# The descriptor space of GpSimd's transfers, 4096 bytes a partition, in a convolution and mixture-of-experts kernel

## The chip, the cores and the metric

The kernel runs on one core of one Trainium2 chip. The metric is the device time of one execution in microseconds (us). Before the change it is 1196.7 us, the median of 3 runs (1196.11 to 1197.26).

## What is computed

The reference chains two parts. The first is a dynamic convolution over 8 sequences of 3584 tokens with 192 values each: every token has 8 heads with 7 weights each, the weights go through a softmax, and each head of 24 values becomes the weighted sum of the token's own values and those of the 6 tokens before it. The second is a mixture of experts with one expert for each token, cut here to what matters:

```
logits = normalized(x) @ normalized(expert_emb).T / tau      # 28672 tokens, 8 experts
expert_idx = argmax(logits); gate_w = its softmax value
for e in range(8):
    h = maximum(x[expert_idx == e] @ w1[e], 0)                # 192 -> 1024
    out[expert_idx == e] = gate_w * (h @ w2[e])               # 1024 -> 192
```

Inputs and output are float32: 8 matrices w1 of 192 x 1024, 8 matrices w2 of 1024 x 192, and an output of 28672 rows of 192 values (768 bytes).

## The kernel before

The tokens are taken in 32 units of 896 (128 partitions by 7). For each unit VectorE forms the convolution's products and sums, ScalarE scales and splits the result into two float16 parts, and SP turns it by a DMA transpose, so that PE can form the logits. VectorE then chooses an expert for each token and counts places, and GpSimd scatters the rows to `lst`, a list in DRAM that has a region for each expert (`scatter`, line 629): one indirect DMA for each of a unit's 7 columns, 128 rows of 776 bytes, 224 such transfers in all.

The experts' layers run over tiles of 256 or 128 rows of one expert. SP fetches a tile's rows from `lst` by a DMA transpose, PE multiplies them with w1 into `h_ps`, ScalarE and VectorE make two float16 parts of the result (`hi`, `lo`), PE multiplies these with w2 into `acc`, and ScalarE scales the sum with the gate into `o`. GpSimd then stores 128 rows of 768 bytes to the output by an indirect DMA (`store`, line 804), 228 transfers in all.

GpSimd also loads the experts' weights at the start (`load`, line 269): four transfers for each expert, of which the fourth, w2, lands as 8 pieces of 768 bytes in each of 128 partitions. With 8 experts these are 32 transfers. The program lets 8 transfers of GpSimd stand open at a time: each one waits on the semaphore of the one 8 before it, unless something else has already waited for that.

```
G_.dma_start(out=self.wa, in_=w1[e, 0:P, :]),
G_.dma_start(out=self.wb[0:D2, :], in_=w1[e, P:D, :]),
G_.dma_start(out=self.wb[D2 : 2 * D2, :], in_=w1[e, P:D, :]),
G_.dma_start(out=self.wc, in_=w2[e].rearrange("(c p) d -> p c d", p=P)),
```

The order of all this on each engine is set before the program is built, by a planner with a cost for each step (`run_steps`). The last 28 tiles take what is left of each expert's rows. Behind them the program computes how many rows are still left and branches (line 1622: `with tc.If(some > 0)`); in this data none are left, and the loops inside are skipped. At the end of that branch the semaphores are set back, GpSimd's own transfers among them (INC_SWDGE_SEM), and at the end of the program (line 1668, `with _tile.TileContext(nc)`) each engine runs a DRAIN and a barrier. Line 1655 makes the program's object; what stands there in the trace is the program's opening, with the same two kinds of instruction.

A transfer that GpSimd issues is written by GpSimd itself, as descriptors, into a space in SBUF that the program sets aside; SP's transfers don't use it. The size of the space is an argument of the program's object; where nothing is given, the library takes 16384 bytes in each partition.

## Time and profile before

| | before |
|---|---|
| median of 3 runs | 1196.7 us (1196.11 to 1197.26) |
| profiled execution | 1197.47 us |
| its span, first to last instruction | 1195.4 us |
| PE (matmul) busy | 1112.6 us, 93% |
| VectorE busy | 1034.4 us, 87% |
| ScalarE busy | 811.0 us, 68% |
| GpSimd busy | 623.7 us, 52% |
| mean granted TensorE clock | 0.976 of full speed |

The page counts what an engine does with data as busy. Register, branch, semaphore and drain instructions are not in these numbers, nor in the list of the costliest groups; they show up where a line's instructions are listed one kind at a time, with a q behind the engine's name (POOLq is GpSimd's, SPq is SP's queue). POOL is GpSimd, DVE is VectorE, ACT is ScalarE. A matmul's line is L66 throughout, that of a helper which records all operations, so groups are told apart by their tiles' names.

### The profile page before, as it was taken

What the parts mean: (1) busy time and instruction counts of PE and PEld (TensorE: products, weight loads), DVE (VectorE), ACT (ScalarE), POOL (GpSimd) and SP (SyncE); (2) the same over time, 40 slices, a digit from 0 to 9 for tenths busy, and PEclk for the clock granted to TensorE, in tenths of its full rate; (3) what the DMA queues carried; (4) which work ended last, traced back from release to release, by engine and by line L of the source; (5) the groups of instructions that cost most, each with busy time, mean ns of one, the idle gap of its engine ahead of it and who ended that gap; (6) DMA issues with size and microseconds to landing.
All of it is one profiled execution on the core that took longest, in us unless ns stands there. A gap on an engine that the chain in (4) does not pass through costs nothing.

```text
span 1195.4 us, 34677 instructions
## 1 busy us (share of the span) xinstructions
PE 1112.6 (93%) x13318; PEld 982.1 (82%) x13318; DVE 1034.4 (87%) x1561; ACT 811.0 (68%) x2076; POOL 623.7 (52%) x566
## 2 busy tenths in 40 slices
PE   4888698679999999999999999999999999999994
PEld 2444487568898899889988989989999988999994
DVE  8999999999999999999999999999984362358882
ACT  1678687669898987988888676776665444444442
POOL 4136262827566685856668675738564632223231
PEclk9988899979999999999999999999999999999998
DMA  9989364566676567755766564744444412211110
GB/s 237 284 172 215 105 158 107 155 139 151 161 164 164 137 162 156 183 153 130 162 158 157 139 159 119 157 116 135 97 97 114 131 49 50 48 43 47 46 45 23
DMA packets 254495, 156.15 MB, mean 131 GB/s; under 512 B 225005, under 2 KB 238565, under 8 KB 251248
## 3 DMA queue, kind: packets, MB, share of 16 engines
q1 hardware_dynamic: 228656, 94.86, 36.9%
q0 software_dynamic: 25664, 58.98, 16.7%
q8 instruction: 106, 1.74, 0.6%
q14 instruction: 69, 0.57, 0.2%
HBM read 62.20 MB, written 46.45 MB: 91 GB/s over the span
## 4 chain that ended last, share of the span: by engine, by line
PE 78%; DVE 12%; issue 3%; DMA 2%; ACT 2%; POOL 1%; DVEq 0%; POOLq 0%; SPq 0%; ACTq 0%
PE h_ps L66 40%; PE acc L66 35%; DVE acc_0x L66 3%; DVE prod_1x L66 2%; DVE prod_0x L66 2%; DVE acc_1x L66 2%; DMA w_t<-in_weight_gen_dram 2%; PE g_ps L66 1%; PE sums_a L66 1%; DMA wlast<-in_moe_w_dram 1%; DVE sums L66 1%; POOL lst L66 1%; ACT hi L66 1%; DVE w_t L66 0%; DVE wall L66 0%
## 5 line engine op out<-in xcount | busy, mean ns | idle before, releaser
L66 POOL DMA_INDIRECT out_dram<-o,meta x228 | 298.3, 1308 | 335.6 <-ACT o L66 192.3
L66 PE MATMUL h_ps<-xt,wall 128*128 128x128 f16 (+2 forms) x5120 | 461.2, 251 | 7.8 <-DVE sums L66 3.4
L66 PEld LDWEIGHTS <-wall 128*128 128x128 f16 (+2 forms) x5316 | 386.0, 98 | 85.7 <-issue 38.0
L66 PE MATMUL acc<-wall,hi 128*128 128x192 f16 x3200 | 411.2, 247 | 0.0
L66 PE MATMUL acc<-wall,lo 128*128 128x192 f16 x1600 | 395.1, 247 | 2.0 <-ACT lo L66 1.9
L66 PEld LDWEIGHTS <-hi 128*128 128x128 f16 x3648 | 328.8, 98 | 11.0 <-issue 3.2
L66 ACT ACTIVATE hi<-h_ps 128x512 f16<-128x512 f32 x456 | 259.3, 598 | 106.3 <-PE h_ps L66 101.1
L66 DVE SCALAR_TENSOR_TENSOR lo<-h_ps,hi 128x512 f16<-128x512 f32 x236 | 154.6, 685 | 109.1 <-ACT hi L66 107.6
L66 ACT ACTIVATE o<-acc,meta 128x192 f32<-128x192 f32 x228 | 88.0, 418 | 166.7 <-issue 148.1
L66 PEld LDWEIGHTS <-lo 128*128 128x128 f16 x1824 | 178.5, 98 | 3.1 <-ACT lo L66 3.1
L66 DVE TENSOR_TENSOR prod_1x<-x_t,w_t 128x1344 f32<-128x1344 f32 x93 | 144.0, 1548 | 0.0
L66 DVE TENSOR_TENSOR prod_0x<-x_t,w_t 128x1344 f32<-128x1344 f32 x93 | 143.9, 1547 | 0.0
L66 ACT ACTIVATE lo<-h_ps 128x512 f16<-128x512 f32 x220 | 127.4, 600 | 10.6 <-PE h_ps L66 8.8
L66 POOL DMA_INDIRECT lst<-row_0x,pos x77 | 102.0, 1324 | 58.0 <-issue 27.8
L66 POOL DMA_INDIRECT lst<-row_1x,pos x77 | 104.9, 1362 | 35.2 <-issue 29.4
L66 POOL DMA_INDIRECT lst<-row_2x,pos x70 | 88.5, 1264 | 48.5 <-issue 47.4
L66 PE MATMUL h_ps<-hi,minus 128*128 128x512 f16 x220 | 72.9, 379 | 7.5 <-ACT hi L66 7.3
L66 DVE TENSOR_TENSOR acc_0x<-acc_0x,prod_1x 128x1344 f32<-128x1344 f32 x45 | 69.8, 1550 | 0.5
L66 DVE TENSOR_TENSOR acc_1x<-acc_1x,prod_1x 128x1344 f32<-128x1344 f32 x45 | 69.6, 1548 | 0.5
L66 DVE TENSOR_TENSOR acc_0x<-acc_0x,prod_0x 128x1344 f32<-128x1344 f32 x45 | 69.8, 1550 | 0.0
L66 DVE TENSOR_TENSOR acc_1x<-acc_1x,prod_0x 128x1344 f32<-128x1344 f32 x45 | 69.6, 1548 | 0.0
L66 PEld LDWEIGHTS <-xT 128*128 128x128 f16 (+1 forms) x918 | 27.8, 97 | 26.4 <-DMA xT<-row_1x 11.8
(217 smaller groups left out, 1365.5 us busy)
## 6 DMA issues: line engine op xcount, KB each, us to landing
x_t<-in_x_dram SPq DMA_DIRECT2D x24, 1248.0 KB
w_t<-in_weight_gen_dram SPq DMA_DIRECT2D x16, 392.0 KB
x_t<-in_x_dram SPq DMA_DIRECT2D x8, 672.0 KB
wall<-in_moe_w_dram POOLq DMA_DIRECT2D x7, 768.0 KB
x_t<-in_x_dram SPq DMA_DIRECT2D x8, 504.0 KB
out_dram<-o,meta POOLq DMA_INDIRECT x228
wall<-in_moe_w_dram POOLq DMA_DIRECT2D x7, 512.0 KB
wall<-in_moe_w_dram POOLq DMA_DIRECT2D x14, 256.0 KB
```

Source lines behind the costliest of these rows:

```text
L66: self.last = self.tc.keep_in_program_order(op(*args, **kwargs))
```

## The change

One argument is given where the program's object is made. All instructions stay as they are, in the same order on each engine; every tile in SBUF starts 12288 bytes lower, since the space lies ahead of the tiles (the first tile's address goes from 16384 to 4096).

```
-    nc = _bacc.Bacc("TRN2", target_bir_lowering=False, num_devices=1)
+    nc = _bacc.Bacc("TRN2", target_bir_lowering=False, num_devices=1, dynamic_dma_scratch_size=4096)
```

## Rows read from the trace of the kernel before

**Rows 1.** The page: span, and busy time of each engine (share of the span)

```profile
span 1195.4 us, 34677 instructions
...
PE 1112.6 (93%) x13318; PEld 982.1 (82%) x13318; DVE 1034.4 (87%) x1561; ACT 811.0 (68%) x2076; POOL 623.7 (52%) x566
```

**Rows 2.** Timeline at the end: start us, us, engine line op out<-in [idle before]

```profile
1179.34 0.42 ACT L66 ACTIVATE o<-acc,meta 128x192 f32<-128x192 f32 x1 [1.38 <-issue]
1180.04 0.97 POOL L66 DMA_INDIRECT out_dram<-o,meta  x1 [1.01 <-ACT o L66]
```

**Rows 3.** Windows of the tail: length, busy us by engine, PEclk, DMA share, GB/s

```profile
1181.10:1183.90 2.80, 0.00 (x0) 0.00 (x0) 0.00 (x0) 0.00 (x0) 0.00 (x0) 0.92 0.14 39
1183.90:1186.10 2.20, 0.00 (x0) 0.00 (x0) 0.00 (x0) 0.00 (x0) 0.00 (x0) 0.50 0.01 4
1186.10:1194.60 8.50, 0.00 (x0) 0.00 (x0) 0.00 (x0) 0.00 (x0) 0.00 (x0) 0.50 0.00 0
```

**Rows 4.** Line 1622: ns min/median/max, first and last start us

```profile
L1622 POOLq INC_SWDGE_SEM  x1: 2240/2240/2240, 1183.9 to 1183.9; - x1
```

**Rows 5.** Line 1668, the program's end

```profile
L1668 SPq EVENT_SEMAPHORE  x14: 17/28/28, 1186.0 to 1195.3; - x14
L1668 POOLq EVENT_SEMAPHORE  x4: 17/17/17, 1194.6 to 1195.3; - x4
L1668 POOLq DRAIN  x3: 46/103/8402, 1186.1 to 1195.1; - x3
L1668 SPq DRAIN  x3: 7/7/13, 1186.8 to 1194.8; - x3
...
L1668 PEldq DRAIN  x2: 8/8/8, 1183.1 to 1194.9; - x2
```

**Rows 6.** Waits of SP's queue from 1170 us on: us, times, longest

```profile
SPq L1668 <- PEq L1668: 8.4, 2, 7.9
```

**Rows 7.** Line 1655, the program's opening

```profile
L1655 POOLq INC_SWDGE_SEM  x1: 27/27/27, 0.1 to 0.1; - x1
...
L1655 POOLq DRAIN  x1: 183/183/183, 0.3 to 0.3; - x1
```

**Rows 8.** Groups of GpSimd: xcount, busy us, mean ns, idle before

```profile
L66 POOL DMA_INDIRECT out_dram<-o,meta x228 | 298.3, 1308 | 335.6 <-ACT o L66 192.3 <-ACT meta L66 72.6 <-issue 15.4
L66 POOL DMA_INDIRECT lst<-row_1x,pos x77 | 104.9, 1362 | 35.2 <-issue 29.4 <-ACT row_2x L66 4.4 <-DVE lo L66 1.1
L66 POOL DMA_INDIRECT lst<-row_0x,pos x77 | 102.0, 1324 | 58.0 <-issue 27.8 <-DVE row_0x L66 17.4 <-ACT wall L66 12.7
L66 POOL DMA_INDIRECT lst<-row_2x,pos x70 | 88.5, 1264 | 48.5 <-issue 47.4 <-DMA lst<-row_1x,pos 0.3 <-ACT sq L66 0.3
L66 POOL DMA_DIRECT2D wall<-in_moe_w_dram x28 | 18.1, 651 | 45.9 <-DMA wall<-in_moe_w_dram 24.6 <-DMA xT<-row_0x 21.3
L66 POOL DMA_DIRECT2D wlast<-in_moe_w_dram x4 | 2.5, 663 | 0.0
```

**Rows 9.** Timeline of GpSimd, an early stretch and a late one

```profile
153.15 1.28 POOL L66 DMA_INDIRECT out_dram<-o,meta  x1 [0.30 <-issue]
155.25 0.97 POOL L66 DMA_INDIRECT out_dram<-o,meta  x1 [0.82 <-ACT o L66]
...
902.29 0.97 POOL L66 DMA_INDIRECT out_dram<-o,meta  x1 [0.30 <-ACT hi L66]
903.56 0.97 POOL L66 DMA_INDIRECT lst<-row_2x,pos  x1 [0.30 <-issue]
```

**Rows 10.** The output's stores: ns min/median/max, first and last start us

```profile
L66 POOL DMA_INDIRECT out_dram<-o,meta x228: 967/1163/2378, 153.2 to 1180.0; - x114
```

**Rows 11.** Waits of GpSimd: us in total, times, longest

```profile
POOL wall L66 <- DMA wall<-in_moe_w_dram: 24.6, 12, 6.3
```

**Rows 12.** Timeline of GpSimd, the first weight loads

```profile
7.43 5.36 POOL L66 DMA_DIRECT2D wall<-in_moe_w_dram  x8
19.06 0.55 POOL L66 DMA_DIRECT2D wall<-in_moe_w_dram  x1 [6.26 <-DMA wall<-in_moe_w_dram]
```

## The prediction

> **What bounds the kernel now.** I read four views, in this order. First the span and the page's busy times. They give a span of 1195.4 us and a PE that is busy for 93% of it [rows 1]; from here to the last stores the kernel is a PE kernel, and GpSimd, the only engine whose transfers the change touches, is busy 52% of the time. A change to GpSimd's transfers therefore gains nothing in the middle, unless it changes what PE waits for. Second, the timeline of the last microseconds: the last store to the output, a GpSimd transfer, starts at 1180.04 and takes 0.97 us [rows 2]. The span ends 14.4 us after that. Third, the windows of this tail: from 1181.1 on no engine is busy, and after 1186.1 the DMA engines move nothing either [rows 3]. The reader is to see that this is no wait for data. Fourth, the queue instructions of the two lines that stand there. On line 1622 GpSimd runs one INC_SWDGE_SEM of 2240 ns from 1183.9 [rows 4]. On line 1668 it runs three DRAINs of 46, 103 and 8402 ns, the first from 1186.1 [rows 5]; a DRAIN of 8.4 us that started later than that would end after the span, so the long one is the first, from 1186.1 to 1194.5. GpSimd's own barrier semaphores start at 1194.6 [rows 5], and SP, whose own DRAIN started at 1186.8, sits there for 7.9 us [rows 5, 6]; the view of waits puts that down to PE, whose DRAIN had begun at 1183.1 [rows 5], so it must be GpSimd. So 2.24 + 8.40 = 10.6 us of the 14.4 us tail are two GpSimd instructions of bookkeeping, with everything else waiting.
>
> The same two instructions stand at the start of the program, before the first transfer. There INC_SWDGE_SEM takes 27 ns and GpSimd's DRAIN 183 ns [rows 7]. Between the two places lie 228 + 77 + 77 + 70 + 28 + 4 = 484 transfers of GpSimd [rows 8]. What these have left behind is 8402 - 183 = 8219 ns of DRAIN and 2240 - 27 = 2213 ns of INC_SWDGE_SEM. It is not data under way: nothing moves in that window [rows 3].
>
> **The change part by part.** No instruction is added, removed or moved; on every engine the two programs have the same instructions in the same order. Two things differ: the space that GpSimd keeps its transfers' descriptors in shrinks from the library's default, 16384 bytes a partition, to 4096, and each tile in SBUF lies 12288 bytes lower. I cost the second at nothing: the same shift for all leaves each tile's place against the others as it was, and no row of the trace lets me price an address.
>
> *The tail, on the path.* My reading is that the space works as a ring whose finished transfers stay on record until room is needed, and that the last DRAIN goes through all that are still on record. With a quarter of the space a quarter can be on record. DRAIN: 183 + 8219 / 4 = 2238 ns, a gain of 6.16 us. INC_SWDGE_SEM, if it goes through the same record: 27 + 2213 / 4 = 580 ns, a gain of 1.66 us. Together 7.8 us. What is late next: SP's semaphores of line 1668 run from 1186.0, that is from the end of INC_SWDGE_SEM, and its two DRAINs end by about 1186.9 [rows 5], 0.9 us later; a DRAIN of 2.2 us on GpSimd is still the last to arrive, so nothing takes the gain back.
>
> The bounds of that ratio. No row shows how many transfers the old space could hold, nor that it was ever full. If it never filled, the new one holds between a quarter and all of what the old one held at the end, and the gain lies between 7.8 us and none. If the space is emptied in one go each time it is full, what is left at the end is a matter of phase: the old one may have stood at only part of its capacity, and then the new one can hold half as much as it, a gain of (8219 + 2213) / 2 = 5.2 us, or next to nothing, where the floor is SP's 0.9 us and the gain 10.6 - 0.03 - 0.9 = 9.7 us. I take the quarter, since 484 transfers are many and a ring that is once full stays near full.
>
> The Trainium skill (DMA: Bandwidth & Descriptors, Terms) gives a descriptor 16 bytes, and the section on the two generation engines puts them into rings in SBUF; its page SBUF — State Buffer, in the section on size, has 16 KiB for them. As an estimate from these pages, a store of 128 rows costs each of 16 DMA engines 8 descriptors and one for the semaphore, so 1024 descriptors hold 113 finished stores and 256 hold 28; both are far below 484, the ratio would be 0.248 and the gain 7.8 us. No run here shows the ring's size.
>
> *The transfers themselves, off the path.* A smaller ring must free old entries sooner: that work moves from the tail into the transfers. The nearest rows say it is not visible there: the second store, at 155.25 us, when few transfers had been sent, takes 0.97 us, and one at 902.29 us, far into the run, takes 0.97 us too [rows 9]. Nor does any of the 228 stores carry a clearing of several microseconds; the longest takes 2.38 us [rows 10]. So I add 0. From above, the two rows could hide 0.01 us each, 4.8 us over 484 transfers, beside some 570 us in which GpSimd idles; from below, a transfer has nothing to win.
>
> *The weight loads.* At the start GpSimd sends 8 weight loads in a row, and after that each load waits for the one 8 before it: 12 waits, 24.6 us [rows 11, 12]. That limit is in the program, and I expect the 4096 bytes to hold eight loads, so the waits stay as they are: 0.
>
> **The sum.** The profiled execution took 1197.47 us, 2.07 us of it outside its span, and 0.77 us more than the median of the runs, 1196.7. Its time becomes 1197.47 - 7.8 = 1189.65, and the median 1188.9; I say 1189.0.
>
> **The rivals.**
>
> *The tail does not depend on the space.* The long DRAIN could cost the same whatever the ring holds: 8219 / 484 = 17 ns for each transfer sent, or a fixed price for having sent any. For it: there is one such DRAIN in the trace, with nothing to compare its length with. Against it: a price for each transfer ever sent needs a record of all 484, which a ring does not keep. Then nothing changes: 1196.7. A form of it lets INC_SWDGE_SEM shrink alone: 1195.0, which is no change by the measure below. And one lets DRAIN shrink alone, 1190.5; that lies in my own case.
>
> *The space becomes too small for the loads under way, and the kernel gets slower.* The place is the weight loads from 7.43 us on [rows 12]. If 4096 bytes do not hold eight of them, of which every fourth is cut into 1024 pieces, GpSimd stops inside a transfer until older ones have landed, and the weights come late to PE. The price: GpSimd waits 24.6 us for landed loads with eight under way [rows 11]; with half as many under way I take the same once more, 24.6 us, all on the path. With the tail's gain: 1196.7 + 24.6 - 7.8 = 1213.5. It decides as soon as two sets of four loads need more than the new space. For it: DMA queues are the fullest just there, so landings are slow (a load sent at 19.06 had waited 6.26 us for one of the first to land [rows 12]). Against it: eight loads are all that the program lets stand open, and the later transfers, 1.27 us or more apart [rows 9], are smaller, so only these loads could feel it.
>
> The Trainium skill speaks for this rival (Perfetto Trace Analysis, DMA Instruction — SWDGE): when a transfer generates more descriptors than the buffer holds, the DMA engines begin before the generation has ended, so GpSimd would have to wait for them. By the 16 bytes of the other page two sets take 168 descriptors an engine, 2688 bytes, as an estimate, and the rule would not bite at 4096.
>
> **How the numbers follow.** What a measurement of this kernel can tell from no change is about 0.2%, 2.4 us. My case, DRAIN shrinks to between almost nothing and half, alone or with INC_SWDGE_SEM: 0.70, from 1187 to 1191.5. The tail does not depend on the space: 0.22, 1195 to 1197.3. Slower by the loads: 0.05. The 0.03 left go to a gain between 1191.5 and 1194, where the old space was hardly full. Faster 0.72, no change 0.22, slower 0.06 with a hundredth for a price of addresses that I don't see. For 8 in 10 the range must take in the second case: 1187.5 to 1197.2; my own case alone is 1187.5 to 1191.5.
>
> **What would show it.** In the profile after: on line 1668 GpSimd's longest DRAIN near 2.2 us in place of 8.4; on line 1622 INC_SWDGE_SEM near 0.6 us in place of 2.24; the last store within a microsecond of 1180.04, since nothing before it has a reason to move; the span's end 6 to 7 us after that store, where it was 14.4. The transfers still take 0.97 us where nothing disturbs them, and GpSimd's wait for weight loads stays at 24.6 us. I am wrong if the DRAIN keeps its 8.4 us (first rival), or if that wait grows and PE's first matmuls of the tiles come later (second). If DRAIN shrinks by another factor than four, the ring keeps something other than a share of its size.

## The result and the profile after

The changed kernel takes 1185.93 us, the median of 4 runs (1184.69 to 1187.02), against 1196.71 us for the kernel before in the same session (1196.11 to 1197.26): a ratio of 0.991, with a 95% interval of 0.9893 to 0.9927. It is 10.8 us faster. The forecast was 1189.0 us, so the sign and the place were right and the gain was larger than I said; the time lies 1.6 us below the low end of the range, 1187.5.

First the page of the changed kernel, which answers to [rows 1]: the instructions are as many, and the busy times hardly move.

```profile
span 1182.7 us, 34677 instructions
...
PE 1114.4 (94%) x13318; PEld 983.5 (83%) x13318; DVE 1034.0 (87%) x1561; ACT 811.6 (69%) x2076; POOL 625.1 (53%) x566
```

Then line 1622 and line 1668 of the changed kernel, as in [rows 4, 5].

```profile
L1622 POOLq INC_SWDGE_SEM  x1: 435/435/435, 1180.3 to 1180.3; - x1
```

```profile
L1668 SPq EVENT_SEMAPHORE  x14: 17/28/28, 1180.7 to 1182.6; - x14
L1668 POOLq DRAIN  x3: 46/103/1052, 1180.8 to 1182.4; - x3
L1668 SPq DRAIN  x3: 7/7/13, 1181.4 to 1182.1; - x3
```

INC_SWDGE_SEM went from 2240 to 435 ns, GpSimd's long DRAIN from 8402 to 1052 ns: 1.81 + 7.35 = 9.16 us, all on the path. SP's longest wait for the others at the end, 7.9 us before [rows 6], is 0.5 us now.

The timeline's last store starts 3.5 us earlier than in [rows 2] and takes the same 0.97 us.

```profile
1176.55 0.97 POOL L66 DMA_INDIRECT out_dram<-o,meta  x1 [1.01 <-ACT o L66]
```

From that store to the end of the span it was 1195.4 - 1180.04 = 15.36 us and is 1182.7 - 1176.55 = 6.15 us. So of the 12.7 us between the two spans 9.2 are the tail. (The spans are those of the two profiled executions, 1197.47 and 1184.69 us; the latter is the shortest of its four, which is why they lie further apart than the medians' 10.8 us.) Nearly all of the other 3.5 lie before the first tile of the experts' layers. Its first matmul is the first time in this row, of the matmuls of a tile's rows with w1 in the kernel before:

```profile
L66 PE MATMUL h_ps<-xt,wall x5120: 216/270/418, 139.2 to 1057.0; 128*128 128x256 f16 x89, 128*128 128x128 f16 x86, 64*128 64x256 f16 x22
```

and in the changed kernel:

```profile
L66 PE MATMUL h_ps<-xt,wall x5120: 216/269/421, 135.9 to 1053.6; 128*128 128x256 f16 x89, 128*128 128x128 f16 x86, 64*128 64x256 f16 x22
```

From the first matmul to the start of the last store it is 1180.04 - 139.2 = 1040.8 us before and 1176.55 - 135.9 = 1040.7 us after. The 3.3 us of the start remain to be told apart from chance.

### The profile page after: what moved, and what is told of

It is laid out like the page before. It is cut to its first block, busy times and chain, and to the rows that moved or that the text cites. A ratio compares the mean times of both kernels' runs of the same rounds, so it can differ in the third digit from the quotient of the medians.

```text
span 1182.7 us, 34677 instructions
## 1 busy us (share of the span) xinstructions
PE 1114.4 (94%) x13318; PEld 983.5 (83%) x13318; DVE 1034.0 (87%) x1561; ACT 811.6 (69%) x2076; POOL 625.1 (53%) x566
## 4 chain that ended last, share of the span: by engine, by line
PE 79%; DVE 16%; issue 2%; ACT 2%; POOL 0%; DVEq 0%; POOLq 0%; ACTq 0%
PE h_ps L66 40%; PE acc L66 35%; DVE acc_0x L66 4%; DVE prod_1x L66 3%; DVE acc_1x L66 3%; DVE prod_0x L66 2%; PE g_ps L66 1%; PE sums_a L66 1%; DVE wall L66 1%; DVE sums L66 1%; DVE w_t L66 1%; ACT hi L66 1%; PE gram L66 0%; DVE row_0x L66 0%; ACT acc_0x L66 0%
```

## The experiments

The experiments tell three theories apart. *Phase*: finished transfers stay on record in the space, the record is emptied in one go when it is full, and the end pays for those that have come since. *Share*: the end pays for a share of the space's size, by some law other than a quarter. *Addresses*: the 3.3 us at the start, or more, come from tiles that lie 12288 bytes lower.

The record can be read off the trace twice, since two instructions grow with it. Let n be the count. Two kernels below clear the record by an early DRAIN, and then send 2 and 7 more stores, which I count as all that is on record at their end; they end with an INC_SWDGE_SEM of 235 and 335 ns and a DRAIN of 221 and 629 ns. So a transfer costs (335 - 235) / 5 = 20 ns in the one and (629 - 221) / 5 = 81.6 ns in the other, which makes INC_SWDGE_SEM = 195 + 20 n ns and DRAIN = 58 + 81.6 n ns. By the first the kernel before ended with (2240 - 195) / 20 = 102 transfers on record, by the second with (8402 - 58) / 81.6 = 102; the changed kernel with (435 - 195) / 20 = 12 and (1052 - 58) / 81.6 = 12. In every kernel here the two instructions give the same n, to within half a transfer.

**More transfers in the old space.** The space stays at 16384 bytes. Behind the last tiles' stores GpSimd sends small transfers of 128 rows to a scratch tensor: 20, 44, or 3 of them (one behind each store, two with 44). They add nothing else to the computation.

```
-    lst16 = lst.bitcast(F16)
+    lst16 = lst.bitcast(F16); spares = []; spare = dram.tile([20, P, 2], I32, name="spare")
...
     class Last(Tile):
+        def store(self, s):
+            super().store(s); [spares.append(G_.behind(G_.dma_start, out=spare[len(spares)], in_=pad[:, 0:2])) for _ in range(1) if len(spares) < 20]
```

> The kernel before (16384 bytes) with 20 more GpSimd transfers, one behind each of the first 20 stores of the last 28 tiles (128 partitions by 8 bytes into a list of their own; the output is untouched). What is read is the last DRAIN of GpSimd and the INC_SWDGE_SEM ahead of it (8402 and 2240 ns before). Theory A, a record that is emptied at once whenever it is full, so that the end depends on how many transfers came after the last emptying: both change, DRAIN up (over 9.5 us) or, if the emptying falls into these 20, far down (under 3 us). Theory B, a full ring that gives up its oldest entry for each new one: no change, 8.4 and 2.2 us. Theory C, a price for each of all transfers sent: 183 + 8219 * 504 / 484 = 8.74 us.

With 20 more the two lines show this:

```profile
L1622 POOLq INC_SWDGE_SEM  x1: 511/511/511, 1186.3 to 1186.3; - x1
```

```profile
L1668 POOLq DRAIN  x3: 46/103/1379, 1186.8 to 1188.7; - x3
```

That is n = 16: twenty more transfers left 86 fewer on record. The one run took 1191.06 us beside 1196.05 of the kernel before (11 runs, 1193.49 to 1198.56), faster by doing more, though the last store starts at 1182.62, 2.6 us later than in [rows 2].

> As the run with 20, with 44 more transfers (two behind each of the first 22 stores of the last 28 tiles). Theory A: DRAIN and INC_SWDGE_SEM move again; if DRAIN rose with 20, it either rises further (over 12 us) or has fallen below 3 us. By the Trainium skill (DMA: Bandwidth & Descriptors, Terms: 16 bytes a descriptor) the old space holds 113 transfers of 9 descriptors an engine; counted from the first transfer, 74 stood there at the end before, so 20 more make 94, and the emptying comes 39 on, which leaves 5 after 44 more: DRAIN under 1 us. Theory B: 8.4 and 2.2 us again. Theory C: 183 + 8219 * 528 / 484 = 9.15 us.

With 44 more:

```profile
L1668 POOLq DRAIN  x3: 46/103/3339, 1196.3 to 1200.2; - x3
```

n = 40: from 20 to 44 more transfers the record rose by the 24 that were added. Its INC_SWDGE_SEM, 991 ns, says 40 as well. The one run took 1202.58 us, 6.5 more than the kernel before, its last store being at 1191.6. Now 102 + 20 - 16 = 106 and 102 + 44 - 40 = 106: in both, 106 left the record. I had put the point of emptying later, after about 39 more transfers; it came before the twentieth.

> The kernel before with 3 more transfers among the last 28 tiles. The counts read so far (102 on record at the end before, 16 after 20 more, 40 after 44 more) say that the record drops 106 at once between the first and the twentieth. With 3 more it should still rise: 105 on record, DRAIN 58 + 82 * 105 = 8.63 us (8.40 before) and INC_SWDGE_SEM 195 + 20 * 105 = 2.30 us (2.24). If it is emptied already at 103 to 105, DRAIN is below 0.4 us.

Three more, and the record still rises: n = 105. The expected 8.63 and 2.30 us came (INC_SWDGE_SEM took 2300 ns):

```profile
L1668 POOLq DRAIN  x3: 46/103/8647, 1259.2 to 1268.4; - x3
```

A share of the size would have left the length as it was with 3, 20 and 44. Phase is what these three show: the record rises one by one to at least 105, and between the 4th and the 20th additional transfer 106 are gone. So the kernel before happens to end near the top, at 102. That they go in a single step, and that none stay behind, is the simplest reading and not shown: a record of up to 122 that keeps up to 16 gives the same counts. With 3 more the one run took 1270.81 us, on a slower chip (see below) where the kernel before took 1265.37 (17 runs).

**The tiles' places.** 4096 bytes, and a filler tile of 12288 bytes a partition ahead of all others, which puts each tile back where it was before (and one small memset on it).

```
-    const = ctx.enter_context(tc.tile_pool(name="const", bufs=1))
+    const = ctx.enter_context(tc.tile_pool(name="const", bufs=1)); filler = const.tile([P, 3072], I32, name="filler"); V.memset(filler[:, 0:1], 0)
...
+    nc = _bacc.Bacc("TRN2", target_bir_lowering=False, num_devices=1, dynamic_dma_scratch_size=4096)
```

> The changed kernel (4096 bytes) with an unused tile of 12288 bytes ahead of all others, so that every other tile lies at the address that it had before. What is read is when the last store starts (1180.04 us before, 1176.55 after) and how fast the first weight loads land. Theory P, the lower addresses of the tiles made the first 60 us shorter: last store near 1180, tail of 6 us, median near 1187.5. Theory R, the smaller space did it: last store at 1176.5 to 1179, median 1185 to 1187 as after. Theory N, neither, the loads' speed differs from one loading of a program to the next: runs of either kind, without a tie to the edit. In all three DRAIN is 1.05 us and INC_SWDGE_SEM 0.44 us.

> The changed kernel once more, timed beside the run with the old tile addresses. Its four runs so far stand in two pairs, 1184.7 and 1185.0, 1186.9 and 1187.0. Theories P and R: 1184.7 to 1187.1 again, all below 1188. Theory N: some runs near 1187.5 or above, where only the tail's 9.2 us (8402 - 1052 + 2240 - 435 ns) are gained. DRAIN 1.05 us and INC_SWDGE_SEM 0.44 us, if these depend on the program alone.

With the old places it took 1185.70 us (5 runs, 1184.83 to 1186.43), ratio 0.9916 [0.9902, 0.993]; the changed kernel on the same chip 1186.58 (6 runs, 1184.14 to 1187.68), 0.9921 [0.9906, 0.9936]. The places do nothing that can be told, and DRAIN and INC_SWDGE_SEM are 1052 and 435 ns in both. The first matmul of the tiles comes at 137.0 and 137.3 us; *addresses* falls.

**The record cleared early, in the old space.** 16384 bytes, and GpSimd runs one DRAIN of its own behind the store of the last tiles' number 20, while other engines have work.

```
     class Last(Tile):
+        def store(self, s):
+            super().store(s); self.j == 20 and G_.behind(G_.drain)
```

> The kernel before (16384 bytes) with one more DRAIN of GpSimd behind the store of the 21st of the last 28 tiles, about 30 us ahead of the end. Theory A (a DRAIN takes some 82 ns for each transfer still on record: (3339 - 1379) / 24 from the runs with 44 and 20 more transfers; and clears the record): with (8402 - 183) / 82 = 100 on record at the end before, the early DRAIN finds about 93 and takes some 7.8 us, beside GpSimd's idle time, and at the end 7 are left: DRAIN 0.75 us, INC_SWDGE_SEM 0.36 us, tail as short as with 4096 bytes, median 1185.5 to 1187.5 though the space is 16384. Theory S (the size of the space itself sets the DRAIN, by going through its bytes): 8.4 us in both places, median above 1196.

> The kernel before (16384 bytes) with a DRAIN of GpSimd behind the store of the 21st of the last 28 tiles, timed beside the changed kernel. If what counts is how many transfers are on record at the end, and not the size of the space: 7 left, DRAIN 0.63 and INC_SWDGE_SEM 0.34 us, a tail 0.5 us shorter than the changed kernel's, and a median within 1 us of it. If the smaller space also gains something ahead of the tail, the changed kernel is faster by 1.6 us or more (10.8 us measured at first, less the tail's 9.2).

> 16384 bytes with a DRAIN behind the store of the 21st of the last 28 tiles; on the calm chip of the first comparisons, if it is met again. If the tail is all of the gain: tail from the last store on 5.7 us, time 9.6 us under the kernel before less what the early DRAIN (9.3 us beside PE) costs, 0 to 1 us; so 0.5 us below to 0.5 us above the changed kernel. If the smaller space gains 1.6 us of its own in the first 140 us: 1.1 us or more above the changed kernel, and the first matmul of a tile at 138 to 139 us where 4096 bytes have it at 136 to 137.5.

These are the same kernel on three chips. On two of them every kernel, that of before too, takes some 70 us more, nearly all of it between the first tile's matmul and the last store, and the kernel before's runs lie 16 us and more apart; so I read the third, the calm one, first. There it took 1185.79 us (5 runs, 1183.45 to 1187.05), ratio 0.9917 [0.9902, 0.9931], like the changed kernel. The early DRAIN, and then the end:

```profile
L66 POOLq DRAIN  x1: 9633/9633/9633, 1151.7 to 1151.7; - x1
```

```profile
L1622 POOLq INC_SWDGE_SEM  x1: 335/335/335, 1181.8 to 1181.8; - x1
```

```profile
L1668 POOLq DRAIN  x3: 46/103/629, 1182.2 to 1183.4; - x3
```

In the timeline GpSimd's work around it reads:

```profile
1151.92 1.56 POOL L66 DMA_INDIRECT out_dram<-o,meta  x1 [5.25 <-ACT meta L66]
1162.21 0.97 POOL L66 DMA_INDIRECT out_dram<-o,meta  x1 [8.73 <-ACT o L66]
```

The early DRAIN ends at 1151.7 + 9.63 = 1161.3, which is 7.85 us after the store at 1151.92 has ended (1153.48). By the rate above that is (7850 - 58) / 81.6 = 95 transfers, and from 1162.21 to the end come 7 more stores: 95 + 7 = 102, the kernel before's count. The end then finds 7. The price of the record is the same in the middle, but there it stands beside other engines' work: from the first matmul (137.5) to the last store (1178.06) it is 1040.6 us, as without it. So on this chip the size of the space costs nothing by itself; what costs is a record that nobody has cleared when the program ends.

On the two slower chips the ends agree (629 and 335 ns, n = 7), but the times don't. On the one, 16384 bytes with the early DRAIN took 1261.07 us (10 runs, ratio 0.9949 [0.9918, 0.9981]) where two kernels shown below, 4096 bytes with an early DRAIN and 2048 bytes, took 1253.37 and 1254.42. On the other it took 1259.93 (12 runs, 0.9964 [0.9927, 1.0]) where the changed kernel took 1249.61 (6 runs, 0.9885 [0.9838, 0.9932]): 15.8 us under the kernel before, and 10.3 us under the old space with the early DRAIN, where I had expected at most 1. So on these chips the tail is not shown to be all of the gain, and a gain of the smaller space's own stands open. The profiles can't settle it. On the second chip the profiled spans are 1252.8 us with the early DRAIN, from one of its shortest runs, and 1253.8 for the changed kernel, from its longest; and from the first tile's matmul to the last store one and the same kernel with the early DRAIN took 1117.0 us on the first chip and 1110.3 on the second, where those with 4096 bytes took 1109.0 to 1110.3.

> The changed kernel (4096 bytes) timed beside the two runs with a DRAIN ahead of the end. DRAIN 1.05 us and INC_SWDGE_SEM 0.44 us as in both earlier profiles (12 transfers on record: 58 + 82 * 12 and 195 + 20 * 12 ns, through the runs with 2 and with 7 left). Its time against the kernel before: the tail's 9.2 us less, and in the rest of the kernel no difference beyond the spread.

> The changed kernel beside it. Tail 6.15 us; the first matmul of a tile between 135.9 and 137.9 us as in the six profiles with 4096 bytes (the six with 16384 have 136.8 to 139.2). Tail alone: 9.2 us under the kernel before; with a gain of its own ahead of the tail: 10.8.

On the calm chip the changed kernel took 1186.25 us (5 runs, 1184.86 to 1188.01), ratio 0.9925 [0.9912, 0.9939].

**Both.** 4096 bytes, and the early DRAIN behind the store of number 25 (`self.j == 25`), the candidate for a still shorter end.

> The changed kernel (4096 bytes) with one more DRAIN of GpSimd behind the store of the 26th of the last 28 tiles, in the pause of some 4 us before the next stores. Theory A: two transfers are on record at the end, DRAIN 183 + 2 * 82 = 0.35 us in place of 1.05 and INC_SWDGE_SEM near 0.26 in place of 0.44; SP's chain of semaphores, 0.8 us behind INC_SWDGE_SEM, now ends later than the DRAIN, so of 0.88 us only some 0.4 to 0.5 us are gained: median 0.4 us under the changed kernel, which its spread of 3 us will hide; the tail from the last store on is 5.7 us where it was 6.15. Theory S: tail as in the changed kernel.

> The changed kernel with a DRAIN behind the store of the 26th of the last 28 tiles: 2 left, DRAIN 0.22 and INC_SWDGE_SEM 0.24 us, tail from the last store on 5.3 us where the changed kernel has 6.15: median 0.85 us under the changed kernel, if the three late microseconds that the early DRAIN takes stay beside PE.

> 4096 bytes with a DRAIN behind the store of the 26th of the last 28 tiles: tail 5.3 us from the last store on, and a time 0.85 us under the changed kernel, if the early DRAIN of 3.0 us delays no store after it.

The calm chip's profile:

```profile
L1622 POOLq INC_SWDGE_SEM  x1: 235/235/235, 1182.9 to 1182.9; - x1
```

```profile
L1668 SPq EVENT_SEMAPHORE  x14: 17/28/28, 1183.1 to 1184.7; - x14
L1668 POOLq DRAIN  x3: 46/103/221, 1183.2 to 1184.5; - x3
L1668 SPq DRAIN  x3: 7/7/13, 1183.9 to 1184.2; - x3
```

n = 2, and GpSimd's DRAIN is over by 1183.4, before SP's first one starts at 1183.9: SP is now the last to arrive. The end is 1184.7 - 1179.13 = 5.6 us after the last store, 0.6 less than in the changed kernel, and 1185.98 us (5 runs, 1184.79 to 1186.78), ratio 0.9916 [0.9903, 0.993], can't be told from it. On the other chips it took 1253.37 (7 runs), 0.9902 [0.9867, 0.9937], and 1251.55 (6 runs), 0.989 [0.9844, 0.9936]. Nothing that I ran beats the changed kernel by more than its spread.

This early DRAIN is not explained by the rate. It starts at 1171.6, takes 3.0 us and ends 1.8 us after the store ahead of it, in all three profiles of this kernel, where 10 transfers on record (12 less the last 2) would give 0.87 us. On the calm chip the DMA engines still move data at 1174.2 to 1174.4, up to 0.2 us before it ends, so it seems to have waited for that store's data. The rate of 81.6 ns is read from the DRAINs at the end, ahead of which the data has landed; the early one of the old space fits it in all three profiles (7.8 us).

**Other sizes.** 2048 and 8192 bytes, by the argument alone.

```
-    nc = _bacc.Bacc("TRN2", target_bir_lowering=False, num_devices=1)
+    nc = _bacc.Bacc("TRN2", target_bir_lowering=False, num_devices=1, dynamic_dma_scratch_size=2048)
```

> The kernel before with 8192 bytes. Theory A (emptied at once when full, a DRAIN pays for what came since): anything between 0.2 and 4.9 us, and INC_SWDGE_SEM must tell the same number left: (DRAIN - 183) / 82 = (INC_SWDGE_SEM - 220) / 20, within one. A DRAIN that grows evenly with the size of the space, through 1.05 us at 4096 and 8.40 at 16384, would be 3.5 us, INC_SWDGE_SEM 1.04 us.

At 8192 bytes one run took 1262.41 us on the first of the slower chips, and the record stood at 47 (INC_SWDGE_SEM 1135 ns):

```profile
L1668 POOLq DRAIN  x3: 46/103/3911, 1255.6 to 1260.1; - x3
```

> The kernel before with 2048 bytes. What is read is GpSimd's wait for weight loads in the first 50 us (24.6 us before), the length of the loads, the last store and the DRAIN. The rival of the prediction, a space too small for the eight loads that the program lets stand open: at 2048 GpSimd stops inside loads or ahead of them, loads of more than 1 us appear or the sixth set's last load is sent later than the 39 to 44 us of the runs so far, and the last store comes after 1180. If 2048 bytes hold what is under way: last store 1176 to 1180 as in all runs. Theory A for the end: at most half of what 4096 bytes can hold is left, DRAIN under 1.4 us and INC_SWDGE_SEM under 0.6 us. By the 16 bytes of the Trainium skill (DMA: Bandwidth & Descriptors, Terms) two sets of loads need 2688 bytes, so the loads would stop.

> 2048 bytes. In the first profile GpSimd waited 32.3 us under no name ahead of weight loads, sent the 20th load at 51.5 us (33 to 44 in all others) and the first matmul of a tile came at 147.0 us (135.9 to 139.2 in all others). If that delay is passed on: the last store 9 to 10 us later than with 4096 bytes, 1186 on the calm chip, and the time 9 us above the changed kernel, about that of the kernel before. If the planner's slack takes it up: within 2 us of the changed kernel.

At 2048 bytes n is 11 (971 and 415 ns), one less than at 4096 and not half: again no share of the size. (That the small spaces are emptied by the same law is argued from this; no run adds transfers to them.) And GpSimd's weight loads change. The view of waits of the calm chip's run, and its timeline from 6 us on:

```profile
POOL wall L66 <- issue: 26.9, 4, 9.1
```

```profile
6.06 4.43 POOL L66 DMA_DIRECT2D wall<-in_moe_w_dram  x7
19.60 2.52 POOL L66 DMA_DIRECT2D wall<-in_moe_w_dram  x4 [9.12 <-issue]
26.15 2.52 POOL L66 DMA_DIRECT2D wall<-in_moe_w_dram  x4 [4.04 <-issue]
34.45 2.51 POOL L66 DMA_DIRECT2D wall<-in_moe_w_dram  x4 [5.78 <-issue]
44.89 0.95 POOL L66 DMA_DIRECT2D wall<-in_moe_w_dram  x1 [7.93 <-issue]
```

Where the kernel before sent 8 loads and then waited for named ones to land [rows 11, 12], GpSimd now stops four times for 26.9 us in all with no releaser that the profile shows, and sends four at a time. These stops stand in place of the named waits, 24.6 us before: in this run GpSimd no longer waits for a load to land, and its 20th load goes out at 44.89 us where the kernel before sent it at 44.05. So the first matmul of the tiles comes at 137.4 us and the time is 1186.05 us (5 runs, 1185.21 to 1187.83), ratio 0.9925 [0.9912, 0.9939]. On the first of the slower chips GpSimd stopped for 32.3 us, the 20th load went out at 51.48 and that first matmul came at 147.0, the latest of all profiles; the time, 1254.42 (10 runs), 0.9896 [0.9863, 0.9929], is still below that of before.

The Trainium skill (Perfetto Trace Analysis, DMA Instruction — SWDGE) has the engines start before generation has ended where a transfer needs more descriptors than the space holds. The stops at 2048 bytes are not that case, since by the 16 bytes of its other page the largest single load, w2 with 65 descriptors an engine, needs 1040 bytes, as an estimate. They fit a space that is full of earlier loads, at a size where the estimate of 2688 bytes for two sets no longer fits in. At 4096 bytes GpSimd's longest idle time of that kind ahead of a load is 0.3 us.

## Why the prediction was right, and where not

**The bound and the place: right.** The gain is in the two GpSimd instructions behind the last store. They gave 9.16 us of the 10.8 us between the medians, and on the two calm chips where both kernels were timed again the difference is 9.5 us (1196.05 - 1186.58) and 9.4 us (1195.67 - 1186.25), so on the calm chips the tail is all of the gain but for what the runs' spread covers.

**The step that failed: the quarter.** I wrote "I take the quarter, since 484 transfers are many and a ring that is once full stays near full". The first half of the reason was right, the second wrong. The ring does not stay full: the runs with 3, 20 and 44 more transfers show 106 leaving it within 17 transfers. What is left at the end is where the count of transfers happens to stand: 102 before, near the top, and 12 after. Both are luck of the count, and with it the size of the gain. The ratio is 12 / 102 = 0.118 and not 0.25, the DRAIN 1052 ns and not 2238, INC_SWDGE_SEM 435 and not 580. The gain of this term was 9.2 us where I had 7.8, and the span's end came 5.2 us after the end of the last store, where I had 6 to 7. The prediction named this way among its bounds ("emptied in one go ... a matter of phase", 5.2 to 9.7 us) and gave it no chance of its own. That the two instructions read one record was right: both say 102, both say 12.

**The range, and the step "nothing before it has a reason to move".** The range's low end, 1187.5, allowed a gain of 9.2 us and nothing else. The tail's 9.16 us alone would have ended there; another 1.6 us took the time out of the range. I had put the rest of the kernel at no change, to within a microsecond at the last store. It doesn't repeat like that: the first tile's matmul starts at 136.8 to 139.2 us in the profiles with 16384 bytes and at 135.9 to 138.3 in those with 4096, two spreads that overlap, so it is not shown to follow the space's size. From there to the last store the profiles from the calm chips, without the two with more transfers, lie within 0.3 us of each other (1040.5 to 1040.8). I read the 1.6 us by which 10.8 exceeds the tail's 9.16 as this spread of the start, since 9.5 and 9.4 us were measured later; why the start varies stays open.

**What is late next: right.** I said SP's semaphores and drains would be 0.9 us behind INC_SWDGE_SEM and that GpSimd would still be last. With n = 12 it is. With n = 2 the rows put SP last, and the end gets only 0.6 us shorter.

**The transfers, at 0: right.** The stores' row in the changed kernel, as [rows 10], has the same median, 1163 ns, and nothing longer than before:

```profile
L66 POOL DMA_INDIRECT out_dram<-o,meta x228: 968/1163/2367, 149.9 to 1176.6; - x114
```

From the first tile to the last store the two kernels differ by 0.1 us. That the smaller space is emptied more often is to be expected; no row shows an emptying.

**The last store "within a microsecond of 1180.04": missed**, at 1176.55, by the start and not by the stores.

**The weight loads and their wait of 24.6 us: cost right, marker poor.** The wait was 19.9 us after, where I expected it to stay. But it was 16.7 us in one of the runs with 16384 bytes and an early DRAIN and 24.6 in another of the same kernel, so it is no sign of anything. The changed kernel still sends eight loads in a row, from 7.13 us on, before it first waits for a landed one, as in [rows 12].

**The first rival** (the tail does not depend on the space) fell. Its argument against itself, that a ring can't keep all 484, held: with 20 more transfers only 16 were on record. **The second rival** (too small for the loads) has a real place, two sets of loads, as at 2048 bytes; its price of 24.6 us on the path was wrong. I had added the stops to the waits for landed loads, and on the calm chip they took the place of these: 26.9 us in all where it was 24.6. There the first tile starts no later than elsewhere, and the time is that of 4096 bytes. On the slower chip the tile started some 10 us later, in one profile.

The Trainium skill's 16 bytes a descriptor (DMA: Bandwidth & Descriptors, Terms) had led to an estimate of 113 stores in the old space. The runs show 106 leaving; the measurement decides, and what makes the difference no run here shows.

## What to carry to other kernels

An instruction at the program's end that grows with what came before it is a term of its own: look at the queue instructions behind the last store, one kind at a time, since no busy time counts them, and clear their record while other engines have work, or keep it small. (The first did as well as the second on the calm chip only; on the slower ones the smaller spaces were 7 to 10 us faster.) Where a length depends on a counter that wraps, forecast its distribution and not a share: here the old DRAIN could have taken anything from about 0.1 to 8.7 us (58 ns, and up to 106 times 81.6 more, if none stay behind), and 20 more transfers made the kernel faster in its one run. And before setting a range, ask how far the part that the change does not touch repeats.

## What the runs showed of the hardware

GpSimd's DRAIN at the end took 81.6 ns for each finished transfer on record and 58 ns besides, INC_SWDGE_SEM 20 ns and 195, over n from 2 to 105. With 16384 bytes the record drops by 106 transfers of 128 rows, and no transfer is seen to pay for it: the longest store took 2.5 us in the runs with more transfers, where 106 at the DRAIN's rate would be 8.6. The two instructions at the opening, 183 and 27 ns [rows 7], are not on these lines. A DRAIN in mid-program ended 7.85 us after the store ahead of it with 95 on record by the count, which is the rate, and 1.8 us after it with 10, which is more than the rate. Where GpSimd ran the long one among the last tiles, 9.6 us on the calm chip, the last store came no later.
